# The second MLP's last product with its operands exchanged

## The chip, the cores and the metric

The kernel runs on one core of a Trainium2 chip. The metric is the device time of one execution in microseconds (us); before the change it is 2472.46 us, the median of 3 runs (2470.71 to 2473.79).

## What is computed

x is 4 x 4096 tokens of 192 channels. Each group of 24 channels is convolved along the sequence with 7 causal taps, whose weights are a softmax. The result, 16384 tokens of 192 channels, goes through two MLPs with 2048 hidden units each:

```python
def _moe_ref(x, w_in, w_out):
    h = x @ w_in
    g = h * np.cos(h)
    return (g @ w_out).astype(np.float32)

def _moe2_ref(x, w_in, w_out):
    h = x @ w_in
    g = np.where(h > 0.0, h, np.exp(np.minimum(h, 0.0)) - 1.0)
    return (g @ w_out).astype(np.float32)

def reference(...):
    x = _attn_ref(x, weight).reshape(B * S, D)      # the convolution
    x = _moe_ref(x, ...)
    return _moe2_ref(x, ...)                        # (16384, 192), float32
```

The weights arrive as float64 and are turned into float32 on the chip.

## The kernel before

**Operands.** Every factor is split into a rounded part h and the rest l (type float32r), and h\*h + h\*l + l\*h are added up in the accumulators. A product has a stationary operand (128 rows by up to 128 columns, which TensorE loads first) and a moving one, whose columns stream through. The tokens are cut into 32 blocks of 512. In all products before the change the weights stand and 512 tokens move, so results have channels on partitions and tokens along the free dimension.

**Steps.** A step takes one block b through one tile f of 128 hidden units (16 tiles) of MLP m. There are 1024 steps: four blocks through the first MLP, the same four through the second, and so on eight times. `step(s)` issues in this order: five first products of step s (`emit_A`, L345), the second activation of step s-1 on ScalarE, the first one of step s, the activation's last operation for s-1 on VectorE (`emit_g`, L378 or L380), the split gh of step s-2 on ScalarE (`emit_hi`, L386), `emit_mid` on VectorE (first MLP only, L364), the rest gl on GpSimd (`emit_lo`, L391), the five second products of step s-5 (`emit_B`, L402 to L406), and one instruction of a chore or of the convolution. If s-5 is a block's last step, its second products are issued earlier, ahead of the split gh. The first 74 steps are ordered by a planner, the others run in the order written.

**Buffers.** The first products write to 4 PSUM buffers (u). The second ones accumulate over the 16 tiles in buffers of a pool of 4 (`ps_a`, acc), of which a block takes two: `a[0]` holds channels 0:128, and `a[1]` has channels 128:192 twice, on its upper and lower 64 partitions, since the stationary `sel` holds the h part of these channels in one half and the l part in the other. gh has 3 buffers, gl 2.

**After a block.** `evac` turns the first MLP's results into operands of the second (L429 to L434). For the second MLP it appends a chore (`store`): ScalarE copies the lower half of `a[1]` (L448), VectorE transposes `a[0]` in squares of 32 (L450), adds the halves (L453) and transposes them (L456), and SP issues six transfers of 32 channels each (L445), which write pieces of 128 bytes.

**Weights.** `prep_w_out` decodes pieces of the output weights in the first 295 us, two instructions a step between the steps' others: VectorE (L148 to L155), GpSimd (L157), then ScalarE's copies and GpSimd's differences (L209 to L213).

Of the kernel before, what the change touches and what calls it, by code (L numbers as in the profile page):

```python
# [36 lines left out]
def conv_then_two_mlps(ctx, tc, x, weight, w_in1, w_out1, w_in2, w_out2, out):  # L37
    """Softmax-weighted causal convolution, then two token-wise MLPs.

    Token t = i * J + j is column (j, i) of a transposed operand: 32 x 32  # L40
    transposes turn segments i into columns when the channels of a partition
    group of 32 are loaded onto it.  Matrix products are float32 products in
    three float32r passes: each operand is split exactly into a rounded part h
    and the rest l, and h*h + h*l + l*h are accumulated (l*l too where its rows
    are free).
    """
# [6 lines left out]
    J = T // Q           # tokens in a segment  # L53
    JB = N // Q          # and of them in a block
# [31 lines left out]
    def channel_masks():  # L86
        # mask[p, n, h]: does channel base + p belong to head h?
# [8 lines left out]
    def softmax_weights():  # L96
# [8 lines left out]
        # Each partition's channel takes its head's weights: 0:128, then 128:192 twice.  # L105
# [14 lines left out]
    for m in (1, 2):  # L120
        for n in ("h", "l", "s"):
            wo[m, n] = const.tile([P, NF, P], F32R, name=f"wo{m}_{n}")
# [3 lines left out]
    def early_tile(dtype):  # L126
        """Where the first MLP's results will stand."""
        zturn.rotate(-1)
        return zt.tile([P, N], dtype, tag=zturn[0], name="early")
# [30 lines left out]
    def prep_w_in(m, half, f0, f1):  # L160
# [14 lines left out]
        else:  # L175
            # The first half of the columns on partitions 0:64, the second on 64:128.
# [21 lines left out]
    def prep_w_out(m, f0, f1):  # L198
# [8 lines left out]
        w, _ = r  # L207
        hi, mid = wo[m, "h"][:, fs, :], wo[m, "s"][:, fs, 0:D2]
        nc.scalar.activation(out=hi, in_=w[:, :, 0:P], func=AF.Copy)  # L209
        nc.scalar.activation(out=mid, in_=w[:, :, P:D], func=AF.Copy)  # L210
        yield
        nc.gpsimd.tensor_tensor(out=wo[m, "l"][:, fs, :], in0=w[:, :, 0:P], in1=f32(hi), op=ALU.subtract)
        nc.gpsimd.tensor_tensor(out=wo[m, "s"][:, fs, D2:P], in0=w[:, :, P:D], in1=f32(mid), op=ALU.subtract)  # L213
        yield

# [1 line left out]
    x_in, ys, xs = {}, {}, {}  # L217

    def load(t, p, b, ch):
# [390 lines left out]
```

## Time and profile before

| | |
|---|---|
| Median of 3 runs | 2472.46 us |
| Span of the profiled execution (the page gives no other time for it) | 2471.2 us |
| TensorE busy | 2354.1 us, 95% |
| TensorE's weight loads (beside products) | 1926.0 us, 78% |
| ScalarE / VectorE / GpSimd busy | 1905.1 / 1607.6 / 1434.3 us |
| Mean granted clock of TensorE | 0.994 |
| Stages | first MLP and second MLP take turns in stages of 64 steps; the first stage begins at 51.8 us and holds the weight preparation |

In the profile PE is TensorE's product, PEld its weight load, DVE VectorE, ACT ScalarE, POOL GpSimd, SP the engine that issues transfers. A product's record is longer than the time by which the next one follows, because products are pipelined: what counts is the time from one start to the next.

### The profile page before, as it was taken

What the parts mean: (1) busy time and instruction counts of PE and PEld (TensorE: products, weight loads), DVE (VectorE), ACT (ScalarE), POOL (GpSimd) and SP (SyncE); (2) the same over time, 40 slices, a digit from 0 to 9 for tenths busy, and PEclk for the clock granted to TensorE, in tenths of its full rate; (3) what the DMA queues carried; (4) which work ended last, traced back from release to release, by engine and by line L of the source; (5) the groups of instructions that cost most, each with busy time, mean ns of one, the idle gap of its engine ahead of it and who ended that gap; (6) DMA issues with size and microseconds to landing.
All of it is one profiled execution on the core that took longest, in us unless ns stands there. A gap on an engine that the chain in (4) does not pass through costs nothing.

```text
span 2471.2 us, 32370 instructions
## 1 busy us (share of the span) xinstructions
PE 2354.1 (95%) x10240; PEld 1926.0 (78%) x10240; DVE 1607.6 (65%) x2373; ACT 1905.1 (77%) x3446; POOL 1434.3 (58%) x1186
## 2 busy tenths in 40 slices
PE   0678999999999999999999999999999999999999
PEld 0455688888888888888888888888888888888887
DVE  3999744994369933797349953599337973387433
ACT  2667878878787787877788787877878777878876
POOL 2777755555555555555555555555555555555555
PEclk9899999999999999999999999999999999999999
DMA  2422111110011100110011100111001100010000
GB/s 66 104 73 75 50 17 19 32 31 5 14 28 27 25 11 11 30 35 16 7 23 28 29 12 13 22 31 28 11 7 34 30 20 8 18 22 14 9 14 14
DMA packets 263733, 65.57 MB, mean 27 GB/s; under 512 B 243336, under 2 KB 252552, under 8 KB 263560
## 3 DMA queue, kind: packets, MB, share of 16 engines
q1 hardware_dynamic: 263560, 63.50, 12.7%
q8 instruction: 80, 1.31, 0.2%
q14 instruction: 93, 0.76, 0.1%
HBM read 29.91 MB, written 12.58 MB: 17 GB/s over the span
## 4 chain that ended last, share of the span: by engine, by line
PE 89%; DVE 7%; SPq 2%; issue 1%; DMA 1%; POOL 0%; ACT 0%; DVEq 0%; POOLq 0%; ACTq 0%
PE u L345 44%; PE acc L405 9%; PE acc L406 9%; PE acc L403 9%; PE acc L404 9%; PE acc L402 9%; DVE w L378 1%; SPq L228 1%; DVE w L364 1%; DVE ew L149 1%; DVE ew L148 1%; DVE ew L154 1%; DVE ew L155 1%; DVE y L291 1%; DMA raw<-in_moe_w_out_dram 0%
## 5 line engine op out<-in xcount | busy, mean ns | idle before, releaser
L391 POOL TENSOR_TENSOR gl<-w,gh 128x512 fp32r<-128x512 f32 x1024 | 1335.9, 1305 | 950.3 <-PE acc L406 630.6
L380 DVE SCALAR_TENSOR_TENSOR w<-w,u 128x512 f32<-128x512 f32 x512 | 352.2, 688 | 696.7 <-ACT w L372 674.4
L386 ACT ACTIVATE gh<-w 128x512 fp32r<-128x512 f32 x1024 | 643.6, 629 | 27.2 <-DVE w L378 13.6
L370 ACT ACTIVATE w<-w 128x512 f32<-128x512 f32 x512 | 323.5, 632 | 216.6 <-DVE w L364 212.5
L355 ACT ACTIVATE w<-u 128x512 f32<-128x512 f32 x512 | 305.6, 597 | 214.3 <-PE u L345 211.3
L405 PE MATMUL acc<-gl,wo_h 128*128 128x512 f32 x1024 | 401.8, 392 | 5.1 <-POOL gl L391 4.9
L378 DVE TENSOR_TENSOR w<-u,w 128x512 f32<-128x512 f32 x512 | 348.6, 681 | 85.3 <-ACT w L370 81.1
L402 PE MATMUL acc<-gh,wo_l 128*128 128x512 f32 x1024 | 400.8, 391 | 0.7 <-ACT gh L386 0.4
L403 PE MATMUL acc<-gh,wo_h 128*128 128x512 f32 x1024 | 400.0, 391 | 0.0
L406 PE MATMUL acc<-gl,wo_s 128*128 128x512 f32 x1024 | 399.9, 391 | 0.0
L404 PE MATMUL acc<-gh,wo_s 128*128 128x512 f32 x1024 | 399.8, 390 | 0.0
L364 DVE SCALAR_TENSOR_TENSOR w<-u,w 128x512 f32<-128x512 f32 x512 | 347.1, 678 | 6.1 <-ACT w L353 5.9
L345 PE MATMUL u<-x,wi_s 128*128 128x512 f32 x1024 | 319.8, 394 | 7.3 <-DMA x<-cl 7.3
L372 ACT ACTIVATE w<-w 128x512 f32<-128x512 f32 x512 | 316.5, 618 | 0.1
L345 PE MATMUL u<-z,wi_s 128*128 128x512 f32 x1024 | 315.7, 390 | 0.0
L353 ACT ACTIVATE w<-u 128x512 int32<-128x512 f32 x512 | 298.6, 583 | 18.3 <-PE u L345 15.5
L291 DVE SCALAR_TENSOR_TENSOR y<-xT,wch,y 128x512 f32<-128x512 f32 x282 | 296.7, 1052 | 0.2
L345 PE MATMUL u<-xh,wi_l 128*128 128x512 f32 x512 | 205.9, 402 | 95.4 <-ACT xh L317 51.8
L405 PEld LDWEIGHTS acc<-gl,wo_h 128*128 128x128 f32 x1024 | 192.8, 188 | 52.2 <-POOL gl L391 12.9
L345 PEld LDWEIGHTS u<-x,wi_s 128*128 128x128 f32 x1024 | 194.4, 190 | 49.1 <-DMA x<-cl 8.0
L402 PEld LDWEIGHTS acc<-gh,wo_l 128*128 128x128 f32 x1024 | 193.0, 189 | 43.0 <-ACT gh L386 2.5
L404 PEld LDWEIGHTS acc<-gh,wo_s 128*128 128x128 f32 x1024 | 193.0, 188 | 40.6
(73 smaller groups left out, 2831.7 us busy)
## 6 DMA issues: line engine op xcount, KB each, us to landing
out_dram<-o SPq DMA_DIRECT2D x192, 64.0 KB
xa<-in_x_dram SPq DMA_DIRECT2D x124, 88.0 KB
raw<-in_moe_w_out_dram SPq DMA_DIRECT2D x32, 192.0 KB
xc<-in_x_dram SPq DMA_DIRECT2D x62, 88.0 KB
x<-ch SPq DMA_DIRECT2D x32, 128.0 KB
x<-cl SPq DMA_DIRECT2D x32, 128.0 KB
z<-z SPq DMA_DIRECT2D x32, 128.0 KB
z<-al SPq DMA_DIRECT2D x32, 128.0 KB
```

The lines of the kernel that those rows point to most:

```text
L345: nc.tensor.matmul(u, lhsT=wi[m, w][:, c], rhs=xx, start=i == 0, stop=i == len(ops) - 1)
L364: paced[0] = nc.vector.scalar_tensor_tensor(out=w, in0=u, scalar=0.25, in1=w.bitcast(I32), op0=ALU.add, op1=ALU.subtract).ins
L370: nc.scalar.activation(out=w, in_=w, func=AF.Sin, scale=6.283185)
L378: nc.vector.tensor_tensor(out=w, in0=u, in1=w, op=ALU.mult)
L380: paced[0] = nc.vector.scalar_tensor_tensor(out=w, in0=w, scalar=-1.0, in1=u, op0=ALU.add, op1=ALU.max).ins
L386: nc.scalar.activation(out=gh, in_=wrk[s], func=AF.Copy)
L391: nc.gpsimd.tensor_tensor(out=gl, in0=wrk.pop(s), in1=f32(gs[s][0]), op=ALU.subtract)
L402: nc.tensor.matmul(a[0], lhsT=l[:, f, :], rhs=gh, start=st, stop=False)
L403: nc.tensor.matmul(a[0], lhsT=h[:, f, :], rhs=gh, start=False, stop=False)
L404: nc.tensor.matmul(a[1], lhsT=sel[:, f, :], rhs=gh, start=st, stop=False)
L405: nc.tensor.matmul(a[0], lhsT=h[:, f, :], rhs=gl, start=False, stop=sp)
L406: nc.tensor.matmul(a[1], lhsT=sel[:, f, :], rhs=gl, start=False, stop=sp)
```

## The change

The second MLP's last product exchanges its operands: 128 tokens of g stand (a piece), and the output weights move, w_h beside w_l in one tile `wo2` (16 tiles x 2 x 192 columns). Per step and piece there is one product of gl with w_h (192 columns) and one of gh with both (384 columns), into one accumulator per piece: columns 0:192 take gl\*w_h + gh\*w_h, columns 192:384 take gh\*w_l. A block has four pieces and takes four accumulators. Results have tokens on partitions; `store` runs at once instead of as a chore, adds the two parts and stores whole rows of 192 channels with four transfers.

```diff
-    for m in (1, 2):
-        for n in ("h", "l", "s"):
-            wo[m, n] = const.tile([P, NF, P], F32R, name=f"wo{m}_{n}")
+    for n in ("h", "l", "s"):
+        wo[1, n] = const.tile([P, NF, P], F32R, name=f"wo1_{n}")
+    wo[2] = const.tile([P, NF, 2, D], F32R, name="wo2")
...
-        hi, mid = wo[m, "h"][:, fs, :], wo[m, "s"][:, fs, 0:D2]
-        nc.scalar.activation(out=hi, in_=w[:, :, 0:P], func=AF.Copy)
-        nc.scalar.activation(out=mid, in_=w[:, :, P:D], func=AF.Copy)
-        yield
-        nc.gpsimd.tensor_tensor(out=wo[m, "l"][:, fs, :], in0=w[:, :, 0:P], in1=f32(hi), op=ALU.subtract)
-        nc.gpsimd.tensor_tensor(out=wo[m, "s"][:, fs, D2:P], in0=w[:, :, P:D], in1=f32(mid), op=ALU.subtract)
+        if m == 1:
+            parts = [(w[:, :, 0:P], wo[m, "h"][:, fs, :], wo[m, "l"][:, fs, :]),
+                     (w[:, :, P:D], wo[m, "s"][:, fs, 0:D2], wo[m, "s"][:, fs, D2:P])]
+        else:
+            parts = [(w, wo[m][:, fs, 0], wo[m][:, fs, 1])]
+        for v, hi, lo in parts:
+            nc.scalar.activation(out=hi, in_=v, func=AF.Copy)
+        yield
+        for v, hi, lo in parts:
+            nc.gpsimd.tensor_tensor(out=lo, in0=v, in1=f32(hi), op=ALU.subtract)
...
+    def emit_B_tokens(b, f, gh, gl):
+        if f == 0:
+            acc[2, b] = [ps_a.tile([P, N], F32, tag="acc", name="acc") for _ in range(N // P)]
+        for q, a in enumerate(acc[2, b]):
+            c = slice(q * P, (q + 1) * P)
+            ops = [
+                (a[:, 0:D], gl[:, c], wo[2][:, f, 0]),
+                (a[:, 0:2 * D], gh[:, c], wo[2][:, f].rearrange("p n d -> p (n d)")),
+            ]
+            if f == 0:
+                ops.reverse()
+            for i, (o, g, w) in enumerate(ops):
+                nc.tensor.matmul(o, lhsT=g, rhs=w, start=f == 0 and i == 0, stop=f == NF - 1 and i == 1)
+        if f == NF - 1:
+            store(b)
+
+    def store(b):
+        o = op.tile([P, N // P, D], F32, tag="o", name="o")
+        for q, a in enumerate(acc.pop((2, b))):
+            nc.scalar.activation(out=o[:, q], in_=a[:, D:2 * D], func=AF.Copy)
+            nc.vector.tensor_tensor(out=o[:, q], in0=a[:, 0:D], in1=o[:, q], op=ALU.add)
+        n = P // Q
+        for jj in range(n):
+            nc.sync.dma_start(out=oseg[:, b * JB + jj:(b + 1) * JB:n, :], in_=o[jj * Q:(jj + 1) * Q])
+
     def emit_B(s):
         m, b, f = steps[s]
         gh, gl = gs.pop(s)
+        if m == 2:
+            return emit_B_tokens(b, f, gh, gl)
...
-        else:
-            chores.append(store(b, a))
-
-    def store(b, a):
...
```

## Rows read from the trace of the kernel before

**Rows 1.** The page, part 1: busy us (share of the span) xinstructions.

```profile
PE 2354.1 (95%) x10240; PEld 1926.0 (78%) x10240; DVE 1607.6 (65%) x2373; ACT 1905.1 (77%) x3446; POOL 1434.3 (58%) x1186
```

**Rows 2.** Windows: the ramp, then stages of second, first, second MLP.

```profile
core 0: us, PE busy (x) PEld busy (x) DVE busy (x) ACT busy (x) POOL busy (x), PEclk, DMA share, GB/s
52.00:287.00 235.00, 175.59 (x634) 122.54 (x635) 233.90 (x400) 167.19 (x392) 171.81 (x196) 0.94 0.34 86
287.00:428.14 141.14, 141.14 (x624) 116.82 (x622) 60.81 (x92) 113.49 (x203) 83.81 (x70) 1.00 0.10 18
428.14:573.20 145.06, 145.06 (x641) 120.14 (x640) 133.90 (x187) 113.86 (x205) 83.65 (x64) 1.00 0.14 27
573.20:718.27 145.07, 145.07 (x641) 120.16 (x640) 54.55 (x81) 116.44 (x201) 82.94 (x64) 1.00 0.08 15
```

**Rows 3.** The page, part 4: chain that ended last, by line.

```profile
PE u L345 44%; PE acc L405 9%; PE acc L406 9%; PE acc L403 9%; PE acc L404 9%; PE acc L402 9%; DVE w L378 1%; SPq L228 1%; DVE w L364 1%; DVE ew L149 1%; DVE ew L148 1%; DVE ew L154 1%; DVE ew L155 1%; DVE y L291 1%; DMA raw<-in_moe_w_out_dram 0%
```

**Rows 4.** Timeline, second MLP: start us, us, engine, line, operation, [idle before].

```profile
1204.47 0.39 PE L402 MATMUL acc<-gh,wo_l 128*128 128x512 f32 x1
1204.47 0.19 PEld L403 LDWEIGHTS acc<-gh,wo_h 128*128 128x128 f32 x1
...
1204.92 0.39 PE L404 MATMUL acc<-gh,wo_s 128*128 128x512 f32 x1
...
1205.15 0.39 PE L405 MATMUL acc<-gl,wo_h 128*128 128x512 f32 x1
```

**Rows 5.** Timeline: TensorE after a stall of 1.3 us.

```profile
94.68 0.19 PEld L405 LDWEIGHTS acc<-gl,wo_h 128*128 128x128 f32 x1 [1.74 <-POOL gl L391]
94.68 0.50 PE L405 MATMUL acc<-gl,wo_h 128*128 128x512 f32 x1 [1.32 <-POOL gl L391]
94.79 0.19 PEld L406 LDWEIGHTS acc<-gl,wo_s 128*128 128x128 f32 x1
...
95.02 0.40 PE L406 MATMUL acc<-gl,wo_s 128*128 128x512 f32 x1
```

**Rows 6.** Timeline: TensorE after an earlier, longer stall.

```profile
60.30 0.29 PEld L345 LDWEIGHTS u<-xh,wi_l 128*128 128x128 f32 x1 [6.18 <-POOL wi_l L173]
...
60.46 0.33 PEld L345 LDWEIGHTS u<-xl,wi_h 128*128 128x128 f32 x1
60.89 0.63 PE L345 MATMUL u<-xl,wi_h 128*128 128x512 f32 x1
...
61.32 0.63 PE L345 MATMUL u<-xh,wi_l 128*128 128x512 f32 x1
```

**Rows 7.** Timeline, second MLP: GpSimd and ScalarE around the same step.

```profile
1201.41 1.28 POOL L391 TENSOR_TENSOR gl<-w,gh 128x512 fp32r<-128x512 f32 x1 [0.97 <-PE acc L406]
...
1204.73 0.60 ACT L355 ACTIVATE w<-u 128x512 f32<-128x512 f32 x1 [0.48 <-PE u L345]
...
1205.35 0.63 ACT L386 ACTIVATE gh<-w 128x512 fp32r<-128x512 f32 x1
```

**Rows 8.** Groups by line and shape: busy us, mean ns, idle before.

```profile
L152 ACT ACTIVATE raw<-raw 128x192 f32<-128x192 uint32 x32 | 12.0, 376 | 10.4 <-DMA raw<-in_moe_w_out_dram 10.4
L155 DVE SCALAR_TENSOR_TENSOR ew<-ew,raw 128x192 f32<-128x192 f32 x32 | 16.2, 505 | 0.0
L291 DVE SCALAR_TENSOR_TENSOR y<-xT,wch,y 128x512 f32<-128x512 f32 x282 | 296.7, 1052 | 0.2
```

**Rows 9.** Timeline: a block's end from the first MLP to the second.

```profile
585.67 0.39 PE L402 MATMUL acc<-gh,wo_l 128*128 128x512 f32 x1
585.75 0.67 DVE L432 SCALAR_TENSOR_TENSOR al<-acc,z 64x512 fp32r<-64x512 f32 x1
```

**Rows 10.** Timeline: the end of the span.

```profile
2464.86 0.40 PE L406 MATMUL acc<-gl,wo_s 128*128 128x512 f32 x1
...
2465.80 3.01 SPq L445 DMA_DIRECT2D out_dram<-o  x6
```

More of the change, by code (lines that the diff above doesn't have):

```diff
@@ L414, in evac @@
         a = acc.pop((m, b))
-        if m == 1:
-            i = b % GROUP
-            if i == GROUP - 1 and len(zpools) < GROUP:
-                for _ in prep:
-                    pass
-                top.close()
-                late.append(ctx.enter_context(tc.tile_pool(name="late", bufs=1)))
-                zpools.append(late[0])
-            z = zpools[i]
-            xh = z.tile([P, N], F32R, tag="zh", name="zh")
-            xl = z.tile([P, N], F32R, tag="zl", name="zl")
-            x3 = z.tile([P, N], F32R, tag="z3", name="z3")
-            x4 = z.tile([P, N], F32R, tag="z4", name="z4")
-            al = op.tile([P, N], F32R, tag="al", name="al")[0:D2]
-            nc.scalar.activation(out=xh, in_=a[0], func=AF.Copy, scale=TWO_PI)
-            nc.scalar.activation(out=x4, in_=a[1], func=AF.Copy, scale=TWO_PI)
-            nc.vector.scalar_tensor_tensor(out=xl, in0=a[0], scalar=TWO_PI, in1=f32(xh), op0=ALU.mult, op1=ALU.subtract)
-            nc.vector.scalar_tensor_tensor(out=al, in0=a[1][0:D2], scalar=TWO_PI, in1=f32(x4[0:D2]), op0=ALU.mult, op1=ALU.subtract)
-            nc.sync.dma_start(out=f32(x3[0:D2]), in_=f32(x4[0:D2]))
-            nc.sync.dma_start(out=f32(x3[D2:P]), in_=f32(al))
-            xs[2, b] = (xh, xl, x3, x4)
-        else:
-            chores.append(store(b, a))
@@ L439, in store @@
-    def store(b, a):
-        cols = lambda ap: ap.rearrange("p (j i) -> p j i", i=Q)
-        j = slice(b * JB, (b + 1) * JB)
-        def put(o, ch0, n):
-            for ch in range(0, n, Q):
-                nc.sync.dma_start(out=oseg[:, j, ch0 + ch:ch0 + ch + Q], in_=cols(o[ch:ch + Q]))
-        lower = op.tile([P, N], F32, tag="al", name="lower")[0:D2]
-        nc.scalar.activation(out=lower, in_=a[1][D2:P], func=AF.Copy)
-        o = op.tile([P, N], F32, tag="o1", name="o")
-        nc.vector.transpose(out=o, in_=a[0])
-        put(o, 0, P)
-        yield
-        nc.vector.tensor_tensor(out=lower, in0=a[1][0:D2], in1=lower, op=ALU.add)
-        yield
-        o = op.tile([P, N], F32, tag="o2", name="o")
-        nc.vector.transpose(out=o[0:D2], in_=lower)
-        put(o, P, D2)
-        yield
+        i = b % GROUP
@@ new lines, in evac @@
+        if i == GROUP - 1 and len(zpools) < GROUP:
+            for _ in prep:
+                pass
+            top.close()
+            late.append(ctx.enter_context(tc.tile_pool(name="late", bufs=1)))
+            zpools.append(late[0])
+        z = zpools[i]
+        xh = z.tile([P, N], F32R, tag="zh", name="zh")
+        xl = z.tile([P, N], F32R, tag="zl", name="zl")
+        x3 = z.tile([P, N], F32R, tag="z3", name="z3")
+        x4 = z.tile([P, N], F32R, tag="z4", name="z4")
+        al = op.tile([P, N], F32R, tag="al", name="al")[0:D2]
@@ new lines, in evac @@
+        nc.scalar.activation(out=xh, in_=a[0], func=AF.Copy, scale=TWO_PI)
+        nc.scalar.activation(out=x4, in_=a[1], func=AF.Copy, scale=TWO_PI)
+        nc.vector.scalar_tensor_tensor(out=xl, in0=a[0], scalar=TWO_PI, in1=f32(xh), op0=ALU.mult, op1=ALU.subtract)
+        nc.vector.scalar_tensor_tensor(out=al, in0=a[1][0:D2], scalar=TWO_PI, in1=f32(x4[0:D2]), op0=ALU.mult, op1=ALU.subtract)
+        nc.sync.dma_start(out=f32(x3[0:D2]), in_=f32(x4[0:D2]))
+        nc.sync.dma_start(out=f32(x3[D2:P]), in_=f32(al))
@@ L461, in prepare @@
+        xs[2, b] = (xh, xl, x3, x4)
     def prepare():
```

## The prediction

> **What bounds the kernel now.** I read the page's busy times first: TensorE has 95% of the span, the next engine 77% [rows 1]. A mean can hide stages with other limits, so I read the windows next. From 52 to 287 us VectorE is busy for 233.9 of 235.0 us while TensorE stands still for 59.4 us: the weights are being prepared, and VectorE is the limit. From 287 us on TensorE is busy for the whole of every window, in the stages of the first MLP and of the second alike [rows 2]. The chain of waits says the same: nearly all of it is products, about 44% the first products (L345) and about 9% each of the five second ones [rows 3]. So from 287 us to the last product, time is the number of products times their pitch, and nothing else can be bought there. A stage of 64 steps (640 products) takes 145.06 us [rows 2]: 226.7 ns a product, 2.267 us a step of ten, 1.133 us for the five second products that the change replaces.
>
> At the granted clock of 1.00, which is 2.4 GHz, 512 columns at one a cycle would take 213.3 ns, so 13.4 ns of the pitch are something else. In the ramp, where the mean granted clock is 0.94 [rows 2], some products after long stalls come 0.43 us apart [rows 6]: by their pitch that is the lower level, 1.2 GHz, and 512 columns at it leave nothing over.
>
> **The price of a weight load.** Each product comes with a load of its stationary operand. In the running stream the load of the next product starts as the present product starts, and not before (1204.47 both), so one load at a time is ahead, and its 0.19 us lie beside a product that lasts longer [rows 4]. What it costs uncovered is seen after a stall: at 94.68 us a load starts, the next load starts at 94.79, which is when the first product's columns begin (that product's record is 0.50 us, 0.11 longer than usual), and the next product at 95.02 [rows 5]. So from a load's start to the first column some 108 ns pass at the full clock (0.11 in the rows); the 0.19 of the record is not what it occupies. At the lower level it is 0.16 us, 60.30 to 60.46 [rows 6].
>
> **The change, part by part.** 512 steps belong to the second MLP (32 blocks of 16). In each, five products of 512 moving columns (2560) become eight: per piece of 128 tokens one of 192 columns (gl beside w_h) and one of 384 (gh beside w_h and w_l), 2304 in all. No row shows a product shorter than 512 columns, so both are bounded.
>
> - 384 columns: if the extra 13.4 ns are per product, 160 + 13.4 = 173.4 ns; if they are per column, 384 x 226.7 / 512 = 170.0. Either covers the next load (108). I take the middle, 171.7.
> - 192 columns: by columns alone 80 + 13.4 = 93.4, or 85.0 in proportion. But the load of this piece's gh may start only when this short product starts and takes 108 ns to the next product's first column, plus the 2 ns by which loads start after products: 110. Upper bound, the nearest row itself: no shorter than a product of 512, 227; between them, load and columns one after the other, 93 + 108 = 201. I take 110, since it is the only one worked out from a load seen without cover.
>
> A step's second products: 4 x (171.7 + 110) = 1126.8 ns for 1133.4, so 6.6 ns less, and over 512 steps 3.4 us less (6.9 less and 0.1 more with the ends of the 384). The ten per cent of columns that are saved are given back to weight loads that no longer have a product long enough to lie beside.
>
> The Trainium skill, "TensorE: Matmul & The Clock Gate", section "Back-to-back issue gap", gives an isolated gap of N / 2.4 + 2.5 ns: 215.8 for 512 columns, where this trace has 226.7. By that rule, eight products would take 4 x (162.5 + 82.5) = 980 ns against 1079 for the five, 99 ns a step less, an estimate of 51 us less in all. It counts no load; the first rival is what it says, priced from rows.
>
> **What else moves.** All of this is off TensorE's path as long as its cover holds:
>
> - gl is now wanted by the first product of a step, not the fourth. GpSimd ends that gl at 1201.41 + 1.28 = 1202.69 and its use was at 1205.15, now 1204.47 [rows 4, 7]: 1.8 us of cover left, cost 0.
> - gh is released by the last product and not by L404, which is 2 x 0.23 us later. ScalarE's split L386 starts just after that release (1205.35, L404 ends 1205.31), and behind it in ScalarE's queue stand the Exp and the next Relu L355. L355 has 0.48 us of idle time before it, waiting for TensorE [rows 4, 7], so ScalarE's pause moves from there to before the split. What L355 starts is wanted by second products five steps later. Cost 0, though the pause is just used up.
> - Evacuation: a 64-partition copy, two transposes and an add of VectorE, spread over later steps, become four copies by ScalarE (376 ns by the nearest row of 128x192) and four adds by VectorE (505 ns by the nearest row of that size) [rows 8], at once in the step in which a block ends. They stand ahead of a gh split on ScalarE (up to 1.5 us late) and, where the first MLP follows, of L364 on VectorE (some 2 us); who waits for these is a product three steps, 6.8 us, later. Cost 0.
> - Accumulators: a block of the second MLP takes all four buffers, and the next block's first products need them a step later. ScalarE is through with L355 about 0.85 us after a block's last products begin (1204.73 + 0.60 against 1204.47), four copies end at 2.35, the last add at 2.86, and the fourth piece is wanted again at 2.27 + 0.84 = 3.11. From the first MLP to the second, L432 ends at 586.42 and the fourth piece is wanted at 585.67 + 0.85 = 586.52 [rows 9]. Cost 0, with 0.1 to 0.25 us of cover; I put 0.3 us in the sum for it.
> - Weight preparation: for each of 16 pieces of the second output weight two copies and two subtractions become one and one. They run beside the VectorE-bound stretch [rows 2], VectorE's part is as it was, so 0. The first 74 steps are ordered by a planner that sees other costs: no row prices that, I keep 3 us on either side.
> - Stores: SP issues four transfers a block for six, with rows of 768 bytes for 128. DMA share is 0.10 to 0.14 in these stages [rows 2], so 0. At the end it counts. Before, six issues run from 2465.80 for 3.01 us and the span ends 2.4 us later [rows 10]. After, the last step's products all wait behind the last gl, so the last one starts 0.6 us later than 2464.86; copy and add take about 0.9, four issues 2.0, landing 2.4: 2471.2 again. Cost 0.
>
> Sum: 2471.2 - 3.4 + 0.3 = 2468.1 us of span. The page gives no time but the span; the three runs have a median 1.3 us above it (2472.46; 2470.71 to 2473.79), so 2469.4. A measurement of this kernel can tell some 0.2% from no change, 4.9 us: this is inside it.
>
> **The rivals.**
>
> 1. *Columns alone set the pitch* (the load of gh runs ahead of the short product after all, or its fixed part overlaps). For it: a load's record and a product's overlap everywhere. Against: no load in the stream starts before the product ahead of it [rows 4, 5]. 4 x (173.4 + 93.4) = 1067 ns, 66 less, 34 us: 2439. In proportion throughout, 4 x 255.0 = 1020, 58 us: 2415.
> 2. *The short product is dear* (slower). Place: the four 192-column products of a step. Each ns over 110 costs 4 x 512 = 2.0 us; beyond about 114 ns the kernel is slower by over 0.2%. Load and columns in series, 201 ns: 4 x (171.7 + 201) = 1491, 357 more, 183 us: 2656. At the rate of a 512-column row, 227: 2709. For it: nothing here shows this type of product at under 512 columns, and the load does not halve with the clock. Against: loads lie wholly beside products in every row.
> 3. *The accumulators run out* (slower). If a convolution tap of VectorE (1052 ns) [rows 8] gets between the adds, the 0.25 us of cover turn into 0.8 us of TensorE at each of 31 block ends: 25 us, 2494.
>
> **How the numbers follow.** Likeliest 0.60, own range 2463 to 2480; within it 0.17 lie under 2467.5, 0.39 inside the 0.2%, 0.04 above. First rival 0.18, second 0.14, third 0.08 (0.06 slower, 0.02 too small to see). Faster 0.17 + 0.18 = 0.35, same 0.39 + 0.02 = 0.41, slower 0.04 + 0.14 + 0.06 = 0.24. The range 2435 to 2500 leaves out the second rival (0.14) and the lower part of the first (0.06).
>
> **What would show it.** After the change the start-to-start time from a gl product to the gh product of its piece should be near 110 ns, from there to the next near 172, and loads of gh should start with the gl products. A stage of the second MLP should take 144.6 us; 141 or less would be the first rival, over 146 the second or third: the second if every step is longer, the third if only the step after a block's end is, with TensorE waiting for VectorE's add. I am wrong if TensorE is idle anywhere between 300 us and the last product.

## The result, and the profile after

The changed kernel takes 2493.91 us, the median of 4 runs (2493.47 to 2494.75); the kernel before, on the same chip, 2473.12 (2470.71 to 2474.04). The ratio is 1.0086, with a 95% interval of 1.0071 to 1.0100: slower by 0.9%. The forecast was 2469.4.

The page of the kernel after: its span, the busy times (the answer to [rows 1]) and the two groups of the exchanged product, that of gh (384 columns) and that of gl (192).

```profile
span 2493.0 us, 35381 instructions
PE 2373.2 (95%) x11776; PEld 2031.0 (81%) x11776; DVE 1597.9 (64%) x2405; ACT 1903.9 (76%) x3528; POOL 1437.2 (58%) x1170
...
L412 PE MATMUL acc<-wo,gh 128*128 128x384 f32 x2048 | 621.6, 360 | 0.2
L412 PE MATMUL acc<-wo,gl 128*128 128x192 f32 x2048 | 513.2, 251 | 0.4 <-POOL gl L396 0.4
```

TensorE is still the bound and is busy 19.1 us longer (2354.1 before), although it streams fewer columns. Its idle time before these two groups is 0.2 and 0.4 us in the whole run: the loss is not in waits for gl or gh. The windows say where it lies. Columns as in [rows 2]: the ramp, then a stage of the first MLP, of the second, and the next of the first:

```profile
53.69:281.68 227.99, 169.90 (x613) 119.00 (x614) 225.96 (x387) 159.96 (x367) 166.28 (x178) 0.95 0.34 87
432.89:578.10 145.21, 145.21 (x657) 121.14 (x657) 131.92 (x188) 114.14 (x208) 84.32 (x64) 1.00 0.14 27
578.10:724.67 146.57, 146.57 (x818) 132.07 (x817) 53.67 (x84) 116.46 (x209) 82.86 (x64) 1.00 0.07 15
724.67:871.56 146.89, 146.21 (x656) 120.87 (x656) 135.16 (x185) 110.89 (x204) 83.44 (x64) 1.00 0.14 27
```

Three things are to be seen. A stage of the second MLP takes 146.57 us with TensorE busy throughout, where 144.65 was forecast and 145.07 was before: its products are slower. The second stage of the first MLP shown takes 146.89, and here TensorE stands still for 0.68 us, which it did in no stage of [rows 2] from 287 us on. And the ramp ends 3.1 us later, with VectorE idle for 2.0 of its 228.0 us; in the kernel before the same stretch is

```profile
51.77:278.58 226.81, 169.31 (x614) 117.96 (x614) 226.67 (x390) 160.44 (x378) 165.63 (x188) 0.95 0.35 87
```

Of these 3.1 us, 1.9 lie ahead of the first product (at 53.69 us instead of 51.77). Three variants of the kernel before that are tried below (the cut, the shortened product, the shifted tiles) have it at 53.3 to 53.5 us, with the same instructions up to there in the same order; so this part is scatter between executions and not the change. The ramp itself is 1.2 us longer.

Summed over the span (21.8 us more), by the starts of the stages:

| stretch | before | after | more |
|---|---|---|---|
| up to the first product of the second MLP (the ramp's end) | 278.58 | 281.68 | 3.1 |
| eight stages of the second MLP, to the last product | 1170.8 | 1184.5 | 13.7 |
| seven stages of the first MLP, of which three long ones | 1015.5 | 1021.5 | 6.0 |
| from the last product to the end | 6.37 | 5.31 | -1.1 |

**The second MLP, product by product.** The pitch of a product is the time from its start to the next one's. In the stream before, each load starts as a product starts [rows 4], so the loads' starts give the pitch too. One step of the kernel after, TensorE's loads (start us, us, engine, line, operation):

```profile
1207.97 0.19 PEld L412 LDWEIGHTS acc<-wo,gl 128*128 128x128 f32 x1
1208.21 0.19 PEld L412 LDWEIGHTS acc<-wo,gh 128*128 128x128 f32 x1
1208.32 0.19 PEld L412 LDWEIGHTS acc<-wo,gl 128*128 128x128 f32 x1
1208.49 0.19 PEld L412 LDWEIGHTS acc<-wo,gh 128*128 128x128 f32 x1
1208.60 0.19 PEld L412 LDWEIGHTS acc<-wo,gl 128*128 128x128 f32 x1
...
1209.17 0.19 PEld L350 LDWEIGHTS u<-zh,wi_l 128*128 128x128 f32 x1
```

and the products among them:

```profile
1208.20 0.25 PE L412 MATMUL acc<-wo,gl 128*128 128x192 f32 x1
1208.29 0.36 PE L412 MATMUL acc<-wo,gh 128*128 128x384 f32 x1
1208.49 0.25 PE L412 MATMUL acc<-wo,gl 128*128 128x192 f32 x1
```

The load of gh starts when the short product of its piece starts, and 0.11 us later the next load starts: read so, the short product lasts as long as that load. From there to the next it is 0.17 to 0.18 us, the long product. The products' own records divide the same time otherwise: the long one's record starts 0.09 us after the short one's, and the next short one 0.20 us later. A record can start while its load is still on the way, as after the stall of [rows 5], and here the long product's record starts some 20 ns before the 108 ns of its load are over. So this text goes by the loads. How a pair's 285 ns divide between its two products is a reading; their sum is not.

Means over some 50 undisturbed steps of the stage from 578 us, by the loads, in ns, by position in the step. A are the five first products, B the second ones; the number of columns is given beside each:

```
before  A(512): 226.3 227.0 226.3 227.1 226.3   B(512): 227.1 226.2 227.1 226.3 227.0            sum 2266.7
after   A(512): 231.7 231.0 231.4 228.5 229.4   192: 108.6 108.4 108.4 108.2  384: 177.8 176.3 176.5 176.5   sum 2292.7
```

The five first products (A), which the change doesn't touch, take 19.0 ns more a step than before, at the same granted clock (1.00 in both windows). A stage of the first MLP starts with five steps whose second products are still those of the second MLP: at 26.0 ns each, these make the 0.13 us by which its undisturbed stages are longer (145.20 for 145.07).

Below, a stream is called settled where products of one length follow each other at a constant pitch, as in [rows 2], and unsettled where they take longer than that, as here.

**The stages of the first MLP.** Three of the seven are long, the second, fourth and sixth. TensorE's products in the first of these (start us, us, ..., [idle before it and who ended it]):

```profile
851.29 0.50 PE L439 MATMUL acc<-gl,wo_h 128*128 128x512 f32 x1
851.63 0.40 PE L440 MATMUL acc<-gl,wo_s 128*128 128x512 f32 x1
852.44 0.50 PE L350 MATMUL u<-xh,wi_l 128*128 128x512 f32 x1 [0.42 <-DVE w L383]
...
855.25 0.50 PE L350 MATMUL u<-xh,wi_l 128*128 128x512 f32 x1 [0.24 <-DVE w L383]
```

From 851.63 to 852.44 are 0.81 us instead of 0.23: a first product waits for a buffer u that VectorE's L383 has still to read. VectorE is late because of something 47 us earlier. GpSimd's subtractions at that place:

```profile
802.27 1.29 POOL L396 TENSOR_TENSOR gl<-w,gh 128x512 fp32r<-128x512 f32 x1 [0.97 <-PE acc L440]
804.83 1.30 POOL L396 TENSOR_TENSOR gl<-w,gh 128x512 fp32r<-128x512 f32 x1 [1.26 <-DVE w L383]
806.81 1.29 POOL L396 TENSOR_TENSOR gl<-w,gh 128x512 fp32r<-128x512 f32 x1 [0.68 <-DVE y L296]
```

and VectorE's convolution taps (one multiply-add of the convolution each) there:

```profile
802.97 1.15 DVE L296 SCALAR_TENSOR_TENSOR y<-xT,wch,y 128x512 f32<-128x512 f32 x1
...
805.24 1.43 DVE L296 SCALAR_TENSOR_TENSOR y<-xT,wch,y 128x512 f32<-128x512 f32 x1
```

The subtractions come every 2.27 us, but the one of 804.83 starts 0.3 us late. The releaser named, L383, is not it: none of the semaphores that the subtraction waits for changes between 804.34 and 804.69. In just that time GpSimd's own sequencer stands for 350 ns between two of its semaphore instructions, where it usually takes 61 ns. Now the subtraction lies further across the next tap, which takes 1.43 us instead of 1.15. How the two are tied can be read from the trace: of the 234 such taps from 430 us on, the 180 that start while GpSimd runs a tensor operation end 0.54 to 0.67 us after that operation does, whenever they started, and the 17 that meet none take 0.74 us. From there VectorE and GpSimd fall behind together (the 35 taps of this stage take 1167 ns in the mean, 1040 in the stage at 432.89) until the pauses of TensorE come. What puts the pause there is the subject of half of the experiments.

### The profile page after: what moved, and what is told of

Same layout as the page of the kernel before. It is cut to its first block, busy times and chain, and to the rows that moved or that the text cites. A ratio compares the mean times of both kernels' runs of the same rounds, so it can differ in the third digit from the quotient of the medians.

```text
span 2493.0 us, 35381 instructions
## 1 busy us (share of the span) xinstructions
PE 2373.2 (95%) x11776; PEld 2031.0 (81%) x11776; DVE 1597.9 (64%) x2405; ACT 1903.9 (76%) x3528; POOL 1437.2 (58%) x1170
## 4 chain that ended last, share of the span: by engine, by line
PE 79%; DVE 14%; ACT 2%; issue 2%; SPq 2%; DMA 1%; POOL 1%; DVEq 0%; POOLq 0%; ACTq 0%
PE u L350 39%; PE acc L412 23%; PE acc L438 3%; PE acc L437 3%; PE acc L436 3%; DVE w L383 3%; PE acc L439 3%; PE acc L440 3%; DVE w L369 3%; DVE y L296 3%; SPq L233 1%; ACT w L375 1%; DVE ew L150 1%; DVE ew L149 1%; DVE ew L155 1%
## 5 line engine op out<-in xcount | busy, mean ns | idle before, releaser
L391 ACT ACTIVATE gh<-w 128x512 fp32r<-128x512 f32 x1024 | 646.2, 631 | 222.8 <-PE acc L412 201.5
L412 PE MATMUL acc<-wo,gh 128*128 128x384 f32 x2048 | 621.6, 360 | 0.2
L412 PE MATMUL acc<-wo,gl 128*128 128x192 f32 x2048 | 513.2, 251 | 0.4 <-POOL gl L396 0.4
L375 ACT ACTIVATE w<-w 128x512 f32<-128x512 f32 x512 | 323.4, 632 | 230.7 <-DVE w L369 226.8
L383 DVE TENSOR_TENSOR w<-u,w 128x512 f32<-128x512 f32 x512 | 349.0, 682 | 102.7 <-ACT w L375 100.1
L412 PEld LDWEIGHTS acc<-wo,gl 128*128 128x128 f32 x2048 | 389.7, 190 | 21.8 <-POOL gl L396 1.2
L412 PEld LDWEIGHTS acc<-wo,gh 128*128 128x128 f32 x2048 | 384.4, 188 | 22.1 <-DVE al L465 0.9
L350 PEld LDWEIGHTS u<-z,wi_s 128*128 128x128 f32 x1024 | 192.7, 188 | 44.1
L439 PE MATMUL acc<-gl,wo_h 128*128 128x512 f32 x512 | 202.8, 396 | 5.7 <-POOL gl L396 5.6
L350 PEld LDWEIGHTS u<-xh,wi_l 128*128 128x128 f32 x512 | 97.0, 190 | 134.6 <-POOL wo_l L218 53.7
L350 PE MATMUL u<-zh,wi_l 128*128 128x512 f32 x512 | 202.6, 396 | 4.2 <-DVE w L383 3.8
```

Source lines behind the costliest of these rows:

```text
L350: nc.tensor.matmul(u, lhsT=wi[m, w][:, c], rhs=xx, start=i == 0, stop=i == len(ops) - 1)
L375: nc.scalar.activation(out=w, in_=w, func=AF.Sin, scale=6.283185)
L383: nc.vector.tensor_tensor(out=w, in0=u, in1=w, op=ALU.mult)
L391: nc.scalar.activation(out=gh, in_=wrk[s], func=AF.Copy)
L412: nc.tensor.matmul(o, lhsT=g, rhs=w, start=f == 0 and i == 0, stop=f == NF - 1 and i == 1)
```

## The experiments

Two theories to begin with, one for each of the two larger terms. For the second MLP: a product cannot be shorter than the load of the next one, and a change of length in the stream makes the products around it dearer; its rivals are that columns alone count, or that the loss belongs to the order of gl and gh. For the first MLP: GpSimd's pause falls in a bad place; its rivals are the evacuation at once, which loads VectorE, and the place at which the convolution starts. "Ratio" is to the kernel before on the same chip, with its 95% interval.

**What a short product costs: the gl product at 128, 256 and 384 columns.**

```diff
-                (a[:, 0:D], gl[:, c], wo[2][:, f, 0]),
+                (a[:, 0:n], gl[:, c], wo[2][:, f].rearrange("p n d -> p (n d)")[:, 0:n]),
```

n = 128. 

> The changed kernel with the gl product narrowed from 192 to 128 moving columns (gl*w_h of channels 128:192 is left out). Load floor: the short product lasts as long as the load it starts, 109 ns from load to load, whatever its columns; time stays at 2494 us (within 3). Columns: 64 columns less at 2.4 GHz are 26.7 ns, four times in 512 steps, 55 us less: 2439.

Measured 2499.99, ratio 1.0113 (1.0098 to 1.0128): 64 columns fewer in 2048 products and 6 us slower, which neither theory had. The short product still takes 108.4 ns, the long one 178 to 180. A pair takes 287 ns for 285, by the loads and by the products' records alike. Columns don't set it; the load of gh does.

n = 256. 

> The changed kernel with the gl product widened from 192 to 256 moving columns (64 columns of gl*w_l are added that were not needed). Load floor: the product outgrows its load only from about 220 columns on, 107 + 13 to 17 = 120 to 124 ns for 109, so 11 to 15 ns four times in 512 steps: 23 to 31 us more, 2517 to 2525. Columns: 26.7 ns each, 55 us more, 2549.

Measured 2511.95, ratio 1.0161 (1.0146 to 1.0176), 5 us under the range. The short product is 117 to 118 ns, just longer than the load, so of the 26.7 ns of 64 columns only 9 are paid; the long product became a little cheaper (174 to 177 for 176 to 178), and a pair takes 292.

n = 384, all eight products of one length. 

> The changed kernel with the gl product as wide as the gh one, 384 columns (gl*w_l is added, which was not needed): eight equal products, no load exposed. It prices 384 columns without short neighbours. Extra time per product in a settled stream: 8 x 173.4 = 1387 ns for 1142, first products at 226.7, 116 us more, 2610. Extra time per column: 8 x 170.0 = 1360, 102 us more, 2596. Unsettled all the same: 8 x 177 = 1416 and first products at 230.5, 140 us more, 2634.

Measured 2634.25, ratio 1.0649 (1.0628 to 1.0671). Loads of one step:

```profile
620.68 0.19 PEld L412 LDWEIGHTS acc<-wo,gl 128*128 128x128 f32 x1
620.91 0.19 PEld L412 LDWEIGHTS acc<-wo,gh 128*128 128x128 f32 x1
621.09 0.19 PEld L412 LDWEIGHTS acc<-wo,gl 128*128 128x128 f32 x1
...
622.15 0.19 PEld L350 LDWEIGHTS u<-zh,wi_l 128*128 128x128 f32 x1
```

Means by position: 177.2 184.7 176.0 181.8, then 173.4 173.5 173.3 173.3. So the settled pitch of 384 columns is 173.3 = 160 + 13.3: the extra 13.4 ns of [rows 2] are per product, not per column. And it takes four products after the change of length until it is reached. The first products behind them are unsettled again (229, 234, 235, 225, 230).

**Does a change of length alone unsettle the stream?** In the kernel before, the product L403 of the second MLP is cut into two of 256 columns:

```diff
-        nc.tensor.matmul(a[0], lhsT=h[:, f, :], rhs=gh, start=False, stop=False)
+        for c in ((slice(0, N),) if m == 1 else (slice(0, N // 2), slice(N // 2, N))):
+            nc.tensor.matmul(a[0][:, c], lhsT=h[:, f, :], rhs=gh[:, c], start=False, stop=False)
```

> The kernel before, with one second product of the second MLP (L403, 512 columns) cut into two of 256 columns with the same weights; nothing else changes. Theory: the pitch of 226.7 ns is that of a settled stream, and a short product unsettles it, so that the step's other nine products take about 231: 9 x 231 + 2 x 120 to 124 = 2319 to 2327 ns for 2267, 27 to 31 us more, 2500 to 2504. Rival: the slower first products after the change come from other engines or the eight loads; here only the cut costs, 2 x 120 - 226.7 = 13 ns a step, 7 us, 2480.

Measured 2490.94, ratio 1.0069 (1.0053 to 1.0086): 17.0 us, between the two. The loads of one step:

```profile
600.68 0.19 PEld L402 LDWEIGHTS acc<-gh,wo_l 128*128 128x128 f32 x1
600.90 0.41 PEld L404 LDWEIGHTS acc<-gh,wo_h 128*128 128x128 f32 x2
601.25 0.19 PEld L405 LDWEIGHTS acc<-gh,wo_s 128*128 128x128 f32 x1
601.36 0.19 PEld L406 LDWEIGHTS acc<-gl,wo_h 128*128 128x128 f32 x1
601.60 0.19 PEld L407 LDWEIGHTS acc<-gl,wo_s 128*128 128x128 f32 x1
601.83 0.19 PEld L345 LDWEIGHTS u<-zh,wi_l 128*128 128x128 f32 x1
```

By position: A 232.6 231.9 226 227 227, L402 226, the halves 115 and 117, then 233 236 228.3. Two halves cost 232 for 226; the five products that follow them cost together some 28 ns more than settled ones, and then the stream is settled again, with the same data, lines and buffers. So it is the cut, and it lasts for about five products; whether by the change of length or by the eleventh product, the next run tells. The step of the kernel after has no two products of one length in a row among its eight, and only five behind them: it never settles.

One product shortened instead of cut, in the kernel before: L403 of the second MLP over 384 of its 512 columns. This leaves out w_h\*gh of the last 128 tokens of each block in that MLP.

```diff
+        c = slice(0, N if m == 1 else 384)
-        nc.tensor.matmul(a[0], lhsT=h[:, f, :], rhs=gh, start=False, stop=False)
+        nc.tensor.matmul(a[0][:, c], lhsT=h[:, f, :], rhs=gh[:, c], start=False, stop=False)
```

> The kernel before, with one second product of the second MLP (L403) over 384 columns for 512 (w_h*gh of a block's last 128 tokens is left out): a change of length in each step, no load exposed, nothing added. Columns alone: 53.3 ns less in 512 steps, 27 us less, 2446. Unsettled stream: the 384 takes 175 to 180 and the next five or six products 4 to 8 ns more each, as after the cut in e5, 25 to 40 ns a step; 7 to 14 us less in all, 2459 to 2466.

Measured 2459.8, ratio 0.9947 (0.9930 to 0.9963). The stage of the second MLP:

```profile
572.20:715.68 143.48, 143.48 (x641) 119.22 (x640) 54.47 (x81) 114.92 (x201) 83.03 (x64) 1.00 0.08 15
```

By the settled pitches, 226.7 - 173.3 = 53.4 ns a step, it would be 145.07 - 64 x 0.0534 = 141.65: more than half of the gain is lost, as forecast. By position: A 227.9 233.0 231.3 226.5 226.7, L402 226.8, the 384 columns 170.4, then 231.1 229.7 236.3. The shortened product gained all of its columns and more; what is lost lies in the products behind it. No product here is near the load's length and the step has ten products as before, and still the next six are dearer, by 29 ns together. So it is the change of length.

**Is it the alternation of gl and gh?** All four gl products first, then the four of gh.

```diff
-        for q, a in enumerate(acc[2, b]):
-            c = slice(q * P, (q + 1) * P)
...
+        for i in range(2):
+            for q, a in enumerate(acc[2, b]):
+                c = slice(q * P, (q + 1) * P)
```

> The changed kernel with a step's four gl products in a row and then its four gh products, the same eight products otherwise. Theory: four short products still expose four loads and still unsettle the stream, so 2494 (within 4). Rival: the alternation unsettles it; in rows of a kind the long products go from 177 to 173.4 ns and the first products from 230.5 to 226.7, 14 + 19 ns a step, 17 us less, 2477.

Measured 2501.12, ratio 1.0112 (1.0097 to 1.0127). Short products 108.3 to 111.6, long ones 179.7 174.0 174.3 175.0: the long ones settle when they stand together, as with 384 columns throughout, but the first products stay dear (229, 234, 235, 225, 230) and the short ones are 3 ns dearer. No gain in grouping.

**The long stages of the first MLP: the form of the weight preparation.** The second weight's copy and subtraction are cut in two again, as they were in the kernel before; the products are those of the kernel after.

```diff
-            parts = [(w, wo[m][:, fs, 0], wo[m][:, fs, 1])]
+            parts = [(w[:, :, c], wo[m][:, fs, 0, c], wo[m][:, fs, 1, c]) for c in (slice(0, P), slice(P, D))]
```

> The changed kernel with the second output weight's split done in two copies and two subtractions again (128 and 64 channels). Theory: the ramp is 3.1 us longer because the planner orders the first steps differently when the preparation has other instructions; it goes back to a first product at 51.8 us and a second MLP from 278.6 us, 2491. Rival: the planner's order differs through the second products of steps 64 to 73; then the ramp stays as after the change, 2494.

Measured 2485.39, ratio 1.0054 (1.0037 to 1.0070): 8.5 us better than the change by the medians (7.9 by the ratios), 6 us under the forecast, which had the ramp alone; and this through work that is over before 300 us. The stage of the second MLP and the one that was long:

```profile
574.48:721.06 146.58, 146.58 (x818) 132.03 (x817) 53.70 (x84) 116.58 (x209) 82.98 (x64) 1.00 0.07 15
721.06:866.26 145.20, 145.20 (x656) 121.15 (x656) 131.70 (x188) 114.06 (x208) 84.64 (x64) 1.00 0.14 27
```

GpSimd and VectorE there, at the step that answers to the late one above (3.6 us earlier, as the stage is):

```profile
800.94 1.31 POOL L396 TENSOR_TENSOR gl<-w,gh 128x512 fp32r<-128x512 f32 x1 [0.96 <-PE acc L440]
803.21 1.30 POOL L396 TENSOR_TENSOR gl<-w,gh 128x512 fp32r<-128x512 f32 x1 [0.96 <-PE acc L440]
```

```profile
801.64 1.15 DVE L296 SCALAR_TENSOR_TENSOR y<-xT,wch,y 128x512 f32<-128x512 f32 x1
...
803.91 1.14 DVE L296 SCALAR_TENSOR_TENSOR y<-xT,wch,y 128x512 f32<-128x512 f32 x1
```

The subtractions keep their 2.27 us and no tap is held longer. The two kernels run alike in this stage for 78 us, to within 10 ns, then one has the pause and the other not. What differs is nothing in the stage, but how many instructions GpSimd has executed before it: 16 more with the preparation cut in two, one for each of its 16 pieces (ScalarE has 16 more too, so GpSimd's count is tried alone below).

**The rivals: VectorE's load, the convolution's place, the planner's.** A chore of three empty places after each block's store, so that no tap falls there:

```diff
+            chores.append(pause())
+
+    def pause():
+        yield
+        yield
+        yield
```

> The changed kernel with an empty chore of as many steps as the old store behind each block of the second MLP, so that the convolution pauses where it paused before. Theory: the three longer stages of the first MLP (146.9 us for 145.2) come from VectorE, which falls behind since the convolution is no longer paused; they go back to 145.1 to 145.2, 5.5 us less, 2488.5. Rival: the copies and adds at a block's end hold VectorE up themselves; then the three stages and the time stay, 2494.

Measured 2498.1, ratio 1.0105 (1.0090 to 1.0120), the wrong way: the long stages got longer.

```profile
724.23:871.84 147.61, 146.90 (x656) 120.66 (x656) 135.92 (x184) 110.31 (x203) 83.00 (x64) 1.00 0.14 27
```

So it is not that the convolution lost its pause. Nor is it the adds of the evacuation: the version above has the same adds and no long stage. The convolution begun two steps later, and 78 planned steps instead of 74:

```diff
-CONV_ON = 80
+CONV_ON = 82
```

> The changed kernel with the convolution resumed two steps later (step 82 for 80); no work is added or removed, and the planner's steps are the same, so the ramp should stay 2 to 3 us longer than before the change. Theory: every other stage of the first MLP is 1.7 us longer because a convolution tap of VectorE and a gl of GpSimd come to lie beside each other there, which hangs on nanoseconds; another alignment changes the pattern: all stages at 145.2 (2488) or more of them long (2497 to 2500). Rival: the new copies and adds at a block's end make these stages long; then the pattern stays, 2494.

```diff
-FREE = 74
+FREE = 78
```

> The changed kernel with 78 steps ordered by the planner for 74. Theory: the ramp's extra time (3.1 us) and the long stages hang on the planner's order and on alignment, so both may move with a change that concerns neither; the second MLP's stages stay at 146.6 us. 2485 to 2494. Rival: both belong to the changed second products and stay, 2494 (within 1).

Measured 2495.48, ratio 1.0088 (1.0073 to 1.0103), and 2494.82, ratio 1.0085 (1.0068 to 1.0102). The same three stages are long (146.95 and 146.91), as the rivals of both said; but the evacuation, the first one's rival, is the same in the version above that has no long stage. With the preparation cut in two and the convolution two steps later together:

> The changed kernel with the old form of the weight's split (as in e4) and the convolution resumed at step 82. Theory: the second MLP's stages stay at 146.6 us, the ramp as in e4; the first MLP's stages show whether e4's 145.2 us survive another alignment: 2485 if they do, up to 2491 with three or four long stages.

Measured 2485.50, ratio 1.0050 (1.0035 to 1.0065): all stages 145.20. The pattern follows the preparation, not the convolution's place.

**GpSimd's count of instructions alone.** Eighteen more instructions on GpSimd at the very start; the preparation is the changed one.

```diff
+    idle = const.tile([P, 1], F32, name="idle")
+    for _ in range(18):
+        nc.gpsimd.memset(idle, 0.0)
```

> The changed kernel with 18 GpSimd memsets of one element per partition, before the first product; nothing else. In the profile of the changed kernel GpSimd's sequencer pauses 350 ns between two of its instructions at one place of every other stage of the first MLP (79.7 us in), the stage lengthens from there, and before the change the pauses fall elsewhere (16.3 and 113.5 us), by some 18 instructions. Theory: it is the pause's place in GpSimd's program that tips VectorE and GpSimd; moved by 18 instructions all stages of the first MLP are 145.2 us, 5.5 to 6 us less, 2488, with the ramp as after the change. Rival: the place is a coincidence and the long stages stay, 2494.

Measured 2523.39, ratio 1.0203 (1.0188 to 1.0219). A miss, and the most useful one. The pauses of TensorE are gone (none over 0.3 us from 309 to 2510 us), yet every stage is longer:

```profile
433.70:582.86 149.16, 149.16 (x657) 121.11 (x657) 131.24 (x188) 117.62 (x208) 88.09 (x64) 1.00 0.14 26
582.86:730.27 147.41, 147.41 (x819) 132.30 (x818) 53.63 (x84) 116.57 (x209) 82.81 (x64) 1.00 0.07 15
```

The edit had done two things. Besides the count, the small tile moves the tiles behind it by 32 bytes, and the products of the first MLP now take 149.16 / 640 = 233.1 ns. So each is tried by itself. The count without a new tile, writing an existing one again:

```diff
-        nc.gpsimd.memset(mask, 1.0)
+        for _ in range(19):
+            nc.gpsimd.memset(mask, 1.0)
```

> The changed kernel with GpSimd's first memset of the masks done 19 times instead of once: 18 instructions more at the start, no tile added. In e11 the long pauses of TensorE were gone, but its added tile moved all tiles behind it by 32 bytes and every product took 233 ns. Theory: with the pause of GpSimd's sequencer moved by 18 instructions and the addresses kept, products of the first MLP stay at 226.7 ns and all its stages are 145.2 us: 5.5 to 6 us less than the changed kernel, 2488. Rival: e11 lost the long stages only because TensorE was slower; then they are back and the time is 2494.

Measured 2488.57, ratio 1.0060 (1.0044 to 1.0077), and the stages:

```profile
432.25:577.45 145.20, 145.20 (x656) 121.25 (x656) 131.78 (x188) 114.11 (x208) 84.47 (x64) 1.00 0.14 27
577.45:724.03 146.58, 146.58 (x818) 132.10 (x817) 53.67 (x84) 116.51 (x209) 82.82 (x64) 1.00 0.07 15
724.03:869.23 145.20, 145.20 (x656) 121.23 (x656) 131.81 (x188) 114.19 (x208) 84.42 (x64) 1.00 0.14 27
```

No long stage is left, by 18 writes of a mask in the first microseconds. GpSimd's pauses are still there, elsewhere in the stages (113.7 and 66.1 us after their start instead of 127.3 and 79.7), where nothing is late by them.

All 16 profiles say the same. The eight kernels in which GpSimd executes 1170 instructions have three long stages, the eight with 1186 or 1188 have none. And if GpSimd's records, its semaphore instructions among them, are numbered in order of time, then all its pauses of over 0.3 us behind a semaphore instruction, from 450 us to the last steps, stand at the same number modulo 128: 8 or 14 pauses in each of the 16 profiles, with no exception. So what moves a pause along the program is how many instructions came before it.

And the 32 bytes without the count, in the kernel before:

```diff
+    const.tile([P, 8], F32, name="shift")
```

> The kernel before with an unused tile of 32 bytes per partition behind the weights, which moves x, z, gh and gl from a multiple of 64 bytes to one of 32, as in e11; no instruction changes. Theory: a moving operand that begins off a multiple of 64 bytes keeps the stream unsettled, so all products take 233 ns as in e11: 6.4 ns x 10 a step in 1024 steps, less the ramp, 60 to 65 us more, 2535. Stages of both MLPs 149.2 us, so the changed second MLP (147.4 in e11) would be the faster one there. Rival: the 233 ns of e11 come from the changed kernel; then 2473.

Measured 2537.33, ratio 1.0256 (1.0241 to 1.0272). Both kinds of stage:

```profile
432.91:582.24 149.33, 149.33 (x641) 120.15 (x640) 129.28 (x187) 118.93 (x205) 91.62 (x64) 1.00 0.14 26
582.24:731.57 149.33, 149.33 (x641) 120.15 (x640) 54.55 (x81) 116.74 (x201) 83.21 (x64) 1.00 0.08 15
```

149.33 / 640 = 233.3 ns a product for 226.7 [rows 2], from an unused tile. The built programs give the addresses: in this run the moving operands (x, z, gh and gl) start 32 bytes beside a multiple of 64, and the stationary ones, the weights, on a multiple of 64 as before. In the kernels before and after all of them start on multiples of 64, so the dearer first products after the change are not this effect. In the run with 18 memsets the same tiles lie beside, while its moving weights wo2 lie on multiples of 64. So in the shifted layout the exchange gains: a stage of the second MLP takes 147.41 us with it (above) and 149.33 without, the whole kernel 2523.39 and 2537.33.

## Why the prediction was wrong, point by point

**The step that failed** is the term of the sum for the pitch of the products that are not short: "384 columns: ... I take the middle, 171.7", and with it the five first products of each step, left at 226.7 because nothing about them was edited. [rows 2] show that pitch only in a stream of products of one length, and the sum carried it into a stream whose length changes nine times in a step of 13 products. Against the forecast, by position, a step has the four long products at 707.1 for 686.8 (+20.3 ns), the five first ones at 1152.0 for 1133.5 (+18.5) and the four short ones at 433.6 for 440 (-6.4): 32.4 ns more, 16.6 us over 512 steps. That is two thirds of the 24.9 us by which the forecast of the span (2468.1) was too low; the rest is mostly the long stages of the first MLP (5.1 us, and 0.8 in the stages behind them) and the 3.1 us ahead of the second MLP, less 1.1 at the end. The bounds of the long product (170.0 to 173.4) held for a settled stream (173.3 measured) and were both below the 176.8 of this one. By the products' own records the two kinds share their time otherwise (91 ns for the short ones, 194 for the long ones, where the prediction looked for 110 and 172), but by either the pair is 3 to 4 ns over its 281.7. That the unsettling comes from the change of length is shown by the cut and by the shortened product in the kernel before; what inside TensorE makes the next five products dearer stays open: no run here tells it.

**The load as floor** was right: 110 ns forecast, 108.4 measured by the loads, and a pair takes the same at 128 columns as at 192. The Trainium skill, "TensorE: Matmul & The Clock Gate", section "LDWEIGHTS (loading the stationary operand)", gives a load as its columns by 1.2 GHz, some 107 ns for 128, which this trace at a granted clock of 1.00 bears out; [rows 6] have 0.16 us at what their pitch of 0.43 us shows to be the lower level (the trace's clock records begin at 75.6 us, so there is no granted clock beside them), which the section doesn't say. The same page's section "Back-to-back issue gap" gives the rule of the prediction's 980 ns for an isolated product, and says that it under-counts short ones since it has no load in it; here the eight products take 1141. That section also gives some 81 ns for each product of 128 columns in a stream of loads and products; in the run with 128 columns, no two loads start less than 108 ns apart from 300 us on.

**The first rival** (columns alone) is false by the pairs with 128 and 192 columns, which take the same time. **The second** was right in its sign and false in its mechanism: the short product is the one term that came out below the sum. The sign that was to show it, a stage of over 146 us with every step longer, came (146.57), but it can't tell a dear short product from dear products around it. **The third** (accumulators run out) is false in its size, and that its price, 2494, is the time measured is a coincidence. Its mechanism is seen in three places, a block's first step after a long stage, where the fourth accumulator's first product comes some 0.2 us late, behind the last instruction (L465) that reads the buffer for the block before:

```profile
884.78 0.25 PE L412 MATMUL acc<-wo,gl 128*128 128x192 f32 x1
885.09 0.19 PEld L412 LDWEIGHTS acc<-wo,gh 128*128 128x128 f32 x1 [0.29 <-DVE al L465]
```

That is not 0.8 us, and not at 31 blocks. The copies and adds were cheaper than the rows taken for them (376 and 505):

```profile
L419 ACT ACTIVATE o<-acc 128x192 f32<-128x192 f32 x128 | 32.0, 343 | 2.4 <-PE acc L412 2.4
...
L420 DVE TENSOR_TENSOR o<-acc,o 128x192 f32<-128x192 f32 x128 | 36.9, 351 | 7.2 <-ACT o L419 4.3
```

**The other waits at 0** held. TensorE was idle for 0.4 us in the whole run ahead of the gl products and for 0.2 ahead of those of gh. The later release of gh makes ScalarE wait ahead of its split (201.5 us in all, for L412), as forecast, and that reaches no product. The stores' stages have a DMA share of 0.07 to 0.14 ([rows 2] have 0.08 to 0.14 before, not 0.10 to 0.14).

**Weight preparation at 0 with 3 us either side** held for the ramp and failed behind it. The ramp itself is 1.2 us longer. In ten profiles with the preparation of the change it takes 227.7 to 228.6 us, in the two with the preparation cut in two 224.4 and 226.0, in the kernel before and its three variants 226.0 to 227.5: it depends on the preparation's form, which is not taken apart further. The 78 planned steps (228.6) show nothing beyond this scatter. What the term didn't have is that 16 instructions fewer on GpSimd moved its pause into the first MLP's convolution: 5.1 us in three stages. That the count of GpSimd's instructions decides is shown by the writes of the mask. That the pause is the fetching of its instructions is only argued: two packets of 8192 bytes on an instruction queue, at 802.02 and 805.38 us, lie near the pause at 804.34, but not in it.

**The end of the span** was right: 5.3 us forecast from the last product's start (0.9 + 2.0 + 2.4), 5.31 measured (1.14 + 1.77 + 2.40), so in part two errors that cancel. The prediction's terms add up to 2464.86 + 0.6 + 5.3 = 2470.8 and not to its 2471.2. The last product, and the four issues of SP:

```profile
2487.72 0.36 PE L412 MATMUL acc<-wo,gh 128*128 128x384 f32 x1
2488.86 1.77 SPq L424 DMA_DIRECT2D out_dram<-o  x4
```

**"TensorE idle anywhere between 300 us and the last product"** was named as what would show the forecast wrong, and it happened: 27 times the next product starts over 0.3 us after the one before it, 5.9 us beyond the pitch in all (3 times and 0.3 us in the kernel before), most of it in the long stages of the first MLP, whose products the change doesn't touch.

No version run here beats the kernel before with all of the work done. What the exchange costs without the accident of the long stages is seen in the three versions that have none and keep the addresses: 11 to 14 us (ratios 1.0050, 1.0054 and 1.0060). In the last of them, with 15.4 us more of span, the stages of the second MLP are 13.0, the time up to it 2.5 (1.6 of it ahead of the first product, so scatter), those of the first MLP 0.9 (145.20 for 145.07, seven times), and the end gives back 1.1.

## What to carry to other kernels

Where TensorE's stream is the bound, price an edit on the products by the stream it makes and not by each product's columns. Two things were worth more here than the columns saved. A short product and the long one behind it took no less than the load between them and the long one's own time, 285 ns with 192 columns as with 128. And a single change of length made the five or six products behind it dearer by 28 or 29 ns in all, edited or not. A saving of columns must be larger than that: 26 ns a step was lost here where 6.6 were to be won. And look at what an edit moves without meaning to: the addresses of moving operands, and an engine's instruction count ahead of a loop.

## What was not expected of the hardware

- Settled and unsettled streams: 226.7 ns for 512 columns among their like, 225 to 236 within six products of one of another length; 173.3 for 384 among their like and 170 to 185 otherwise.
- Moving operands moved by 32 bytes: 233.3 ns instead of 226.7 for 512 columns at the same granted clock, 64.6 us of span in the kernel before. In the fast layouts they start at multiples of 64 bytes, in the slow one 32 bytes beside, with the stationary operands left where they were.
- GpSimd's sequencer stands for some 350 ns at fixed places of its program, multiples of 128 records apart. In the kernel before, the pauses lie 16 and 113.5 us into a stage and cost nothing; 79.7 us in, one pause costs TensorE 1.7 us. A convolution tap of VectorE that starts while a subtraction of GpSimd runs ends some 0.55 us after it, so a subtraction that is 0.3 us late makes the tap 1.43 us long instead of 1.15, and later ones up to 1.86.
